# A planner that reckons TensorE's clock from its own order, and passes that shift the priorities of kinds of pieces

## The chip, the cores and the metric

The kernel runs on one core of one Trainium2 chip. The metric is the device time of one execution in microseconds (us), as the median of several. The core has five instruction queues that run side by side, each in the order in which its instructions were written: PE (TensorE, matrix products and transpositions), DVE (VectorE), ACT (ScalarE), POOL (GpSimd) and SP (SyncE, which here issues the transfers). A queue whose next instruction waits for data holds everything behind it.

## The reference

Sliding-window attention with four sink keys, followed by a gated feed-forward block that mixes over the sequence. Four batches, eight heads, 768 positions, 64 per head; d_model 512, d_ff 1024.

```python
scores = scale * np.matmul(q, k.transpose(0, 1, 3, 2))
keep = is_sink | in_window            # 4 sinks, window of 128
a = softmax(where(keep, scores, -1e9))
x = (a @ v), heads side by side       # B, S, 512
h = np.maximum(x @ w_in, 0.0)
u, v = h[..., :512], h[..., 512:]
v_n = (v - mean) / sqrt(var + 1e-6)
v_s = einsum('ts,bsd->btd', w_spatial, v_n) + b_spatial
out = (u * v_s) @ w_out
```

w_in and w_out come as 64-bit floats and are decoded on the chip. Products are made from halves (a high and a low part of 16 bits, or of a reduced 32-bit type), three matmuls for each.

## The kernel before

The sequence is cut in six tiles t of 128 rows and the heads in two halves hf, so that a batch b has twelve "halves" of attention, 48 in all (counted here from 0: half 0 is b 0, t 0, hf 0). For each half PE makes the scores (tile `sc`, L969 for batch 0 and L975 for the others), DVE masks them and takes the row maximum (L980, writes `pexp`, `nm`), ACT makes the exponentials (L985), and the weights are transposed: in batch 0 on PE (`tr`, L1013; a small one for the sinks at L1022) with a copy to `pT` on ACT or DVE (L1017), in the other batches by a DMA (L1047). Then PE multiplies by v (`av`, L1101 and L1093 in batch 0, L1085 to L1087 in the others). DVE divides (L1112, writes `x`), x is split in two halves and transposed by a DMA (L1129, `xT`). The feed-forward block has four kinds of products on PE, all at L686: `ps_v` (x by the second half of w_in; 12 matmuls, 24 pieces), `ps_u` (the first half; 12 matmuls, 48 pieces), `ps_s` (w_spatial by the normalised v; 18 matmuls, 48 pieces) and `ps_o` (w_out; 12 matmuls, 24 pieces).

At the start the weights are read and decoded: `dec` is the raw w_in, `w` and `wtmp` are its parts on ACT (L741, L743), DVE and POOL put them together (L739 to L752), a maximum over all of w_in (`ps_row`, `ps_col` are the two small PE steps of such a maximum) gives the scale, and `win` are the scaled halves (L654 on ACT, L675 on DVE). `junk` are ACT passes that sum absolute values for the scales of v and w_spatial.

None of this order is written by hand. `Plan` collects the pieces (`add`) with a rank, the engines that may do them, a time for each and the keys that they read and write. `prepare` finds the dependences. `forward` lays the pieces out one after the other in a model of the five queues and the buffers: of the pieces that could go on next it takes the one with the smallest start plus a small penalty for its priority. `backward` goes through the same pieces from the end and returns for each the latest start; these are the priorities of the next pass. `order` repeats this 40 times and keeps the pass with the earliest end. In the model PE's pieces took 1.9 times as long up to a fixed moment, 33:

```python
if e == "PE" and b < COLD:
    d *= COLD_TIMES
```

The instructions are then written out in the order of that pass, and on the chip each queue runs its own share in that order.

Of the kernel before, what the change touches and what calls it, by code (L numbers as in the profile page):

```python
# [299 lines left out]
NAMES = ("PE", "d", "a", "p", "SP")  # L300


class Plan:
# [8 lines left out]

    def add(self, rank, engines, time, f, reads=(), writes=(), dma=None, shared=False):
        self.pieces.append((rank, len(self.pieces), engines, time, f, tuple(reads), tuple(writes), dma, shared))

    def prepare(self):
        ps = self.ps = sorted(self.pieces, key=lambda x: x[:2])
        n = len(ps)
        before, seen, users = [set() for _ in ps], {}, {}
        for i, (_, _, _, _, _, reads, writes, _, _) in enumerate(ps):  # L320
# [36 lines left out]

    def forward(self, prio):
        ps, n = self.ps, len(self.ps)
# [5 lines left out]
        free = dict.fromkeys(NAMES, 0.0)  # L365
        port, moved = 0.0, DMA_START
        open_ = [i for i in range(n) if not missing[i]]
# [18 lines left out]
        while open_:  # L386
            least = min(prio[i] for i in open_)
            best = None
            for i in open_:
                t = room(i)  # L390
                if t is None:
                    continue
                t = max(t, ready[i])
                if ps[i][7] and not ps[i][5]:
                    t = max(t, moved - QUEUED)
                c = None
                for e, d, shared in self.choices[i]:
# [6 lines left out]
                key = (c[1] + min(AHEAD_MOST, AHEAD * (prio[i] - least)), prio[i], i)  # L404
                if best is None or key < best[0]:
                    best = (key, c)
            if best is None:
                raise RuntimeError("plan: no piece can go on: " + str([(ps[i][0], ps[i][5], ps[i][6]) for i in open_[:16]])
                                   + str({r: [(b, b and left[b]) for b in h] for r, h in slots.items()}))
            (_, _, i), (_, t, e, d) = best  # L410
            _, _, _, _, f, reads, writes, dma, shared = ps[i]
# [64 lines left out]

    def order(self):
        self.prepare()
        prio, best, self.ends = [p[0] for p in self.ps], None, []
        for _ in range(PASSES):  # L480
            end = self.forward(prio)
            self.ends.append(end)
            if best is None or end < best[0]:
                best = (end, self.last)
            prio = self.backward()
        self.end, (start, length, lag, engine, order, follow) = best
        return [(self.ps[i][4], engine[i]) for i in order]


# [50 lines left out]
def fast_path(tc, st, scalars, qk, v, v0, vs, w_in, w_sp, b_sp, w_out, out):  # L540
# [7 lines left out]
    with (  # L548
# [149 lines left out]
        def all_max(rank, name, cols):  # L698
# [19 lines left out]
            plan.add(rank, "d", 0.15, a, [("mx", name)], [("m", name)])  # L718
            plan.add(rank, "PE", 0.2, b, [("m", name)], [("ps_row", name)])
            plan.add(rank, "d", 0.27, c, [("ps_row", name)], [("1", name)])  # L720
# [226 lines left out]
        def scores(i, b, t, hf, h2, r, n):  # L947
# [35 lines left out]
            def exped(q):  # L983
# [3 lines left out]
            keys = [(f"kslot{kslot(b, x)}", (b, x)) for x in ((t, t - 1) if t else (t,))]  # L987
            plan.add(r, "PE", 0.19 + n / 2 * (0.45 if whole(b) else 0.35), product,
                     ([("qkraw", (b, t)), ("k0room", 0)] if whole(b) else [("qp", (b, t))]) + keys, banks)
            for q in range(n):  # L990
# [10 lines left out]
        def weights_whole(i, b, t, hf, r):  # L1001
# [4 lines left out]
            for k in range(n // 4):  # L1006
# [11 lines left out]
                plan.add(r, "PE", 0.44, turn, [("pexp", i, h) for h in hs], [("tr", (i, k))])  # L1018
                plan.add(r + WHEN["copy0"], ENGINES["pT copy"], {"a": 0.54, "d": 0.63}, copy, [("tr", (i, k))], [("pT", i, k)])
            if t > 1:  # L1020
# [11 lines left out]
                plan.add(r, "p", 0.17, pick_sinks, [("pexp", i)], [("sk", i)])  # L1032
                plan.add(r, "PE", 0.11, turn_sinks, [("sk", i)], [("tr", (i, "s"))])
                plan.add(r + WHEN["copy0"], ENGINES["pT copy"], {"a": 0.23, "d": 0.22}, copy_sinks, [("tr", (i, "s"))],
# [30 lines left out]
        def attend(i, b, t, hf, r):  # L1065
# [48 lines left out]
            if whole_values(b):  # L1114
                plan.add(r, "PE", (0.55 if t > 1 else 0) + 0.225 * n + 0.15, product_whole, [("pT", i)] + [v_key(kt) for kt in tl_]
                         + ([("sinkT", i), ("p16", ("v", hf), 1)] if t > 1 else []), [("av", (b, t), hf)])
            else:
                plan.add(r, "PE", 0.03 * 3 * n + 0.12, product,
                         [("pT", i)] + vkeys + ([(f"vsink{vsk}", b)] if t > 1 else []), [("av", (b, t), hf)])
            if hf == 0:  # L1120
# [13 lines left out]
        def v_half(b, t, r):  # L1134
# [40 lines left out]
            vn = lambda: tl("vn", i)  # L1175
            plan.add(r, "PE", 2.62, product, [("xT", (b, t // 2), t % 2), ("win", 1)], [("ps_v", i)])
            plan.add(r + WHEN["v relu"], ENGINES["v relu"], {"a": 0.59, "d": 0.6}, relu, [("ps_v", i), ("icv", b)], [("vr", i)])
# [7 lines left out]
        def u_half(b, c0, d, r):  # L1185
# [10 lines left out]

            plan.add(r, "PE", 1.33, product, [("xT", (b, c0)), ("win", 0)], [("ps_u", i)])
            plan.add(r + WHEN["u relu"], "a", 0.36, lambda e: nc.scalar.activation(  # L1198
# [4 lines left out]
        def s_piece(b, c0, d, r):  # L1203
# [20 lines left out]
            g2 = lambda: tl("g2", i)  # L1224
            plan.add(r, "PE", 2.0, product, [("vn", (b, s)) for s in range(NT)] + [("wsp", s) for s in range(NT)], [("ps_s", i)])
            plan.add(r + WHEN["gate"], "d", 0.4, gate, [("ps_s", i), ("b_bc", 0)], [("g", i)])
# [4 lines left out]
        def o_piece(b, c0, k, r):  # L1231
# [11 lines left out]
            r0 = TC * c0 + k * P  # L1243
            plan.add(r, "PE", 2.83, product, [("g2", (b, c0, d)) for d in range(KC)] + [("wout", c) for c in range(KC)], [("ps_o", i)])
            plan.add(r + WHEN["o copy"], "a", 0.5, lambda e: nc.scalar.copy(tl("ob", i), tl("ps_o", i)), [("ps_o", i)], [("ob", i)])  # L1245
# [102 lines left out]
```

## Time and profile before

| | |
|---|---|
| time, median of 3 runs | 441.69 us (440.2 to 443.3) |
| profiled execution, its own time | 440.84 us |
| span of that execution | 439.1 us |
| mean granted clock of TensorE in it | 0.974 |
| PE busy | 417.5 us, 95% of the span |
| DVE busy | 324.0 us, 74% |
| ACT busy | 272.3 us, 62% |
| POOL busy | 174.9 us, 40% |
| DMA | 59.98 MB, mean 137 GB/s |

The span is what lies between the first and the last instruction of the execution; the time has 1.8 us more around it. A busy PE is not PE at its peak: its matmuls take twice as long where the granted clock is 0.50 (1.2 GHz) as where it is 1.00 (2.4 GHz). A granted clock of 0.51 or 0.97 is a mean over a stretch that has some of both. In the trace views a row with "xN" stands for N instructions in a row; the bracket behind it says how long the engine had been idle and what ended that. The fp32 matmuls of batch 0 stand as two instructions each.

### The profile page before, as it was taken

What the parts mean: (1) busy time and instruction counts of PE and PEld (TensorE: products, weight loads), DVE (VectorE), ACT (ScalarE), POOL (GpSimd) and SP (SyncE); (2) the same over time, 40 slices, a digit from 0 to 9 for tenths busy, and PEclk for the clock granted to TensorE, in tenths of its full rate; (3) what the DMA queues carried; (4) which work ended last, traced back from release to release, by engine and by line L of the source; (5) the groups of instructions that cost most, each with busy time, mean ns of one, the idle gap of its engine ahead of it and who ended that gap; (6) DMA issues with size and microseconds to landing.
All of it is one profiled execution on the core that took longest, in us unless ns stands there. A gap on an engine that the chain in (4) does not pass through costs nothing.

```text
span 439.1 us, 9829 instructions
## 1 busy us (share of the span) xinstructions
PE 417.5 (95%) x3669; PEld 327.4 (75%) x3669; DVE 324.0 (74%) x925; ACT 272.3 (62%) x583; POOL 174.9 (40%) x227
## 2 busy tenths in 40 slices
PE   2689999999999999999999999999999999999994
PEld 1467787777877878767778877868778778688883
DVE  1998799869899997779897875779996656144430
ACT  2898979978876765488865554778663443232121
POOL 4324346645865652255536713445531213000000
PEclk9957999969999999999999999999999999999999
DMA  7999721355876845279958664366543614500111
GB/s 212 331 353 311 222 68 30 98 120 158 176 176 157 210 116 173 65 165 229 209 111 176 132 144 115 74 166 167 115 79 100 144 58 56 92 1 13 37 49 55
DMA packets 117928, 59.98 MB, mean 137 GB/s; under 512 B 100240, under 2 KB 103920, under 8 KB 117872
## 3 DMA queue, kind: packets, MB, share of 16 engines
q1 hardware_dynamic: 117872, 59.27, 53.7%
q8 instruction: 31, 0.51, 0.5%
q14 instruction: 25, 0.20, 0.2%
HBM read 28.58 MB, written 6.29 MB: 79 GB/s over the span
## 4 chain that ended last, share of the span: by engine, by line
PE 84%; DVE 8%; DMA 4%; ACT 2%; issue 1%; SPq 0%; DVEq 0%; ACTq 0%
PE ps_s L686 18%; PE ps_o L686 15%; PE ps_u L686 15%; PE ps_v L686 12%; PE sc L975 7%; PE av L1101 5%; PE sc L969 2%; PE tr L1013 2%; DVE pexp L980 2%; PE av L1085 2%; DMA dec<-w_in 2%; PE av L1087 2%; PE av L1086 2%; DMA wsp<-qk_t 1%; PE av L1093 1%; DVE vring L675 1%
## 5 line engine op out<-in xcount | busy, mean ns | idle before, releaser
L686 PE MATMUL ps_s<-wsp,vn 128*128 128x256 f16 x864 | 100.8, 273 | 0.0
L686 PEld LDWEIGHTS <-vn 128*128 128x128 f16 x864 | 82.7, 98 | 12.5 <-issue 0.7
L985 ACT ACTIVATE pexp<-pexp,nm 128x260 f32<-128x260 f32 (+1 forms) x192 | 81.9, 484 | 14.9 <-DVE nm L980 14.8
L686 PE MATMUL ps_o<-wout,g 128*128 128x512 f32 x288 | 71.0, 400 | 0.6 <-DVE g L1219 0.3
L686 PE MATMUL ps_u<-xT,win 128*128 128x256 f16 x576 | 68.9, 273 | 0.5 <-ACT vr L1150 0.5
L686 PE MATMUL ps_v<-win,xT 128*128 128x512 f16 x288 | 66.7, 381 | 0.0
L686 PEld LDWEIGHTS ps_o<-wout,g 128*128 128x128 f32 x288 | 52.9, 188 | 13.9 <-DVE g L1219 0.8
L686 PEld LDWEIGHTS <-win 128*128 128x128 f16 x576 | 54.6, 98 | 10.6 <-issue 2.4
L668 DVE TENSOR_TENSOR p<-pexp,p 128x1024 f16<-128x1024 f32 (+2 forms) x57 | 48.8, 876 | 3.6 <-ACT p L652 2.7
L686 PEld LDWEIGHTS <-xT 128*128 128x128 f16 x288 | 27.2, 98 | 30.8 <-issue 1.8
L1219 DVE SCALAR_TENSOR_TENSOR g<-ps_s,isc,b_bc 128x256 f32<-128x256 f32 x48 | 23.1, 481 | 34.8 <-PE ps_s L686 33.6
L668 POOL TENSOR_TENSOR x<-x,x 128x512 f16<-128x512 f32 x24 | 32.8, 1365 | 34.3 <-ACT x L652 33.8
L652 ACT CAST g<-g 128x256 fp32r<-128x256 f32 x35 | 14.0, 403 | 46.1 <-DVE g L1223 44.4
L975 PE MATMUL sc<-kring,qp 64*128 64x260 f32 (+1 forms) x432 | 36.2, 300 | 0.0
L975 PEld LDWEIGHTS sc<-kring,qp 64*128 64x128 f32 x432 | 28.8, 189 | 7.1 <-issue 4.1
L1198 ACT ACTIVATE u<-ps_u,icu 128x256 f32<-128x256 f32 x48 | 22.6, 470 | 18.0 <-PE ps_u L686 18.0
L1245 ACT COPY ob<-ps_o 128x512 f32<-128x512 f32 x24 | 14.0, 585 | 30.2 <-PE ps_o L686 30.2
L1166 POOL TENSOR_TENSOR rs<-rs,mhalf 128x1 f32<-128x1 f32 x24 | 17.7, 738 | 36.6 <-DVE rs L1160 34.6
L652 ACT CAST p<-pexp 128x1024 f16<-128x1024 f32 (+2 forms) x52 | 31.4, 637 | 0.5
L1156 DVE BATCH_NORM_STATS2 st<-vr 128x6 f32<-128x512 f32 x24 | 16.5, 690 | 18.2 <-ACT vr L1150 18.2
L1085 PE MATMUL av<-vring,pT 128*128 128x65 f16 x264 | 27.7, 193 | 0.0
L1086 PE MATMUL av<-vring,pT 128*128 128x65 f16 x264 | 27.6, 193 | 0.0
(151 smaller groups left out, 773.9 us busy)
## 6 DMA issues: line engine op xcount, KB each, us to landing
qkraw<-qk_t SPq DMA_DIRECT2D x18, 512.0 KB, 4.4
out<-ob SPq DMA_DIRECT2D x24, 256.0 KB, 2.2
vraw<-v_s SPq DMA_DIRECT2D x18, 256.0 KB, 4.5
dec<-w_in SPq DMA_DIRECT2D x8, 512.0 KB, 8.4
dec<-w_out SPq DMA_DIRECT2D x4, 512.0 KB, 5.6
wsp<-qk_t SPq DMA_DIRECT2D x6, 256.0 KB, 6.1
qkraw<-qk_t SPq DMA_DIRECT2D x6, 256.0 KB, 4.0
wsp<-w_sp_t SPq DMA_DIRECT2D x3, 384.0 KB, 9.5
```

The lines of the kernel that those rows point to most:

```text
L652: nc.scalar.copy(o, x)
L668: eng[e].tensor_tensor(out=o, in0=x, in1=hi, op=ALU.subtract)
L686: nc.tensor.matmul(o, a, m, start=(i == 0), stop=(i == n - 1))
L975: nc.tensor.matmul(o, qp[rows, qi, hp, :], keys(kring[:, ki], rows), start=(m == 0), stop=(m == 2))
L985: nc.scalar.activation(po, po, AF.Exp, bias=nm()[:, h2 + q:h2 + q + 1], scale=-1.0)
L1085: nc.tensor.matmul(o[:, h], ph, vh, start=(t < 2 and j == 0), stop=False)
L1086: nc.tensor.matmul(o[:, h], ph, vl, start=False, stop=False)
L1101: nc.tensor.matmul(o[:, h], pT[:, q * P:(q + 1) * P], v_whole(kt)[:, g:g + D + 1], start=(t < 2 and j == 0), stop=(j == nb - 1 and (t < 2 ...
L1156: nc.vector.bn_stats(s6, vr())
L1166: nc.gpsimd.tensor_tensor(out=vals["rs", i], in0=vals["rs", i], in1=mhalf, op=ALU.pow)
L1198: plan.add(r + WHEN["u relu"], "a", 0.36, lambda e: nc.scalar.activation(tl("u", (b, c0))[:, d, :], tl("ps_u", i)[:, :TC], AF.Relu, scale= ...
L1219: nc.vector.scalar_tensor_tensor(out=g(), in0=tl("ps_s", i)[:, :TC], scalar=vals["s", "sp"][1], in1=b_bc[:, t0:t0 + TC], op0=ALU.mult, op1 ...
```

## The change

Three things are changed, all in the planner; no operation of the kernel is added or taken away.

- A class `Clock` stands in for the fixed moment. `add` takes the moving columns of each PE piece, `forward` hands each piece that it lays out on PE to the clock, and the clock says for the next whether it runs at full or half speed (factor 2.0).
- `order` no longer repeats 40 like passes and takes the best. It goes through 22 steps. Each step runs some passes, and the first pass of a step adds to every priority a pseudo-random shift, one for each kind of piece and one for each piece, from a seed in the table. The order is that of the last pass. If a pass gets stuck, `settle` repeats it with a stronger pull to the priorities.
- The model times of scores on PE are changed: in batch 0 from 1.09 to 1.10 (0.62 for t 0), in the others from 0.89 to 0.93 (0.79 for t 0).

```diff
-COLD, COLD_TIMES, DMA_START, DMA_LAND = 33.0, 1.9, 0.5, 1.5
+COLD_TIMES, DMA_START, DMA_LAND = 2.0, 0.5, 1.5
+SPELL, ENOUGH = 3.41333, 3030.0
-PASSES = 40
+PASSES = ((3000009, 582, 0, 4), (3000010, 417, 0, 3), (3000020, 470, 158, 4),
...
+class Clock:
+    def __init__(self):
+        self.start, self.sum, self.full = -SPELL, 0.0, False
+    def at(self, t):
+        start, sum_, full = self.start, self.sum, self.full
+        while start + SPELL <= t:
+            start, sum_, full = start + SPELL, 0.0, sum_ >= ENOUGH
+        return start, sum_, full
+    def time(self, t, d):
+        return d if self.at(t)[2] else d * COLD_TIMES
+    def run(self, t, d, columns):
+        self.start, self.sum, self.full = self.at(t)
+        end, p = t + d, t
+        while end > self.start + SPELL:
+            q = self.start + SPELL - p
+            self.full = self.sum + columns * q / d >= ENOUGH
+            p = self.start = self.start + SPELL
+            self.sum = 0.0
+        self.sum += columns * (end - p) / d
+def scatter(seed, i):
+    x = (seed * 2654435761 + i * 40503 + 12345) & 0xFFFFFFFF
...
+    return (x & 0xFFFF) / 65536.0 + (x >> 16) / 65536.0 - 1.0
...
-                    if e == "PE" and b < COLD:
-                        d *= COLD_TIMES
+                    if e == "PE":
+                        d = clock.time(b, d)
...
+            if e == "PE":
+                clock.run(t, d, columns)
...
+        self.end = self.settle([p[0] for p in self.ps])
+        for seed, of_kind, of_piece, passes in PASSES:
+            for k in range(passes):
+                prio = self.backward()
+                if k == 0:
+                    prio = [x + of_kind / 100.0 * scatter(seed, kind[p[1]]) + of_piece / 100.0 * scatter(seed + 7919, 100000 + p[1])
+                            for x, p in zip(prio, self.ps)]
+                self.end = self.settle(prio)
+        start, length, lag, engine, order, follow = self.last
...
+    def settle(self, prio):
+        ahead, most = AHEAD, AHEAD_MOST
+        while True:
+            try:
+                return self.forward(prio, ahead, most)
+            except Stuck:
+                ahead, most = 2 * ahead, 4 * most
...
```

What this does to the program is a new order on every queue, and another engine for some of the pieces that may go to several. Three places follow.

The first is ACT at the start of the program, before the change (w and wtmp are the decode of w_in, pexp the exponentials):

```order
L741 ACTIVATE w_181<-dec 128x512
L743 ACTIVATE wtmp<-dec 128x512
L985 ACTIVATE pexp<-pexp,nm 128x128 x4
L741 ACTIVATE w_207<-dec 128x512
L741 ACTIVATE w_211<-dec 128x512
L743 ACTIVATE wtmp<-dec 128x512
L985 ACTIVATE pexp<-pexp,nm 128x128 x4
```

And with the change:

```order
L1046 ACTIVATE pexp<-pexp,nm 128x128 x4
L802 ACTIVATE w_200<-dec 128x512
L804 ACTIVATE wtmp<-dec 128x512
L1046 ACTIVATE pexp<-pexp,nm 128x128
L802 ACTIVATE w_217<-dec 128x512
L1046 ACTIVATE pexp<-pexp,nm 128x128
L1079 COPY pT<-tr 128x512
```

The exponentials of half 0 moved ahead of the first decode; those of half 1 stay behind it.

The second is SP at the start, before the change (`wsp` holds k of batch 0 at that time, `qkraw` its q):

```order
L924 DMA wsp<-qk_t 128x4x128
L680 DMA qkraw<-qk_t 128x512
L680 DMA dec<-w_in 128x1024 x3
L924 DMA wsp<-qk_t 128x4x128
L680 DMA qkraw<-qk_t 128x512
L680 DMA dec<-w_in 128x1024
L886 DMA vring<-v_ones 128x2x520 x2
```

And with the change:

```order
L985 DMA wsp<-qk_t 128x4x128
L741 DMA qkraw<-qk_t 128x512 x2
L985 DMA wsp<-qk_t 128x4x128
L741 DMA dec<-w_in 128x1024 x3
L947 DMA vring<-v_ones 128x2x520
L741 DMA dec<-w_in 128x1024
L947 DMA vring<-v_ones 128x2x520
```

The q and k of the second tile, 256 KB each, moved ahead of the first three loads of w_in.

The third is PE up to the first `ps_v`. Before the change, from the transpositions of half 2:

```order
L1013 MATMUL tr<-ident,pexp 128x128 x8
L713 MATMUL ps_col<-allmax_352,ones 128x1
L1101 MATMUL av<-vring,pT 128x65 x4
L969 MATMUL sc<-wsp,qkraw 128x260 x4
L1101 MATMUL av<-vring,pT 128x65 x8
L1013 MATMUL tr<-ident,pexp 128x128 x8
L706 MATMUL ps_row<-ident,allmax_m 1x128
L969 MATMUL sc<-wsp,qkraw 128x260 x4
L1101 MATMUL av<-vring,pT 128x65 x8
L1013 MATMUL tr<-ident,pexp 128x128 x8
L1022 MATMUL tr<-ident,sk 16x128
L686 LDWEIGHTS xT
```

And with the change, from the transpositions of half 3:

```order
L1075 MATMUL tr<-ident,pexp 128x128 x8
L1030 MATMUL sc<-wsp,qkraw 128x260 x4
L1163 MATMUL av<-vring,pT 128x65 x8
L1075 MATMUL tr<-ident,pexp 128x128 x8
L767 MATMUL ps_row<-ident,allmax_m 1x128
L1084 MATMUL tr<-ident,sk 16x128
L1163 MATMUL av<-vring,pT 128x65 x8
L1030 MATMUL sc<-wsp,qkraw 128x260 x4
L1075 MATMUL tr<-ident,pexp 128x128 x8
L1084 MATMUL tr<-ident,sk 16x128
L747 LDWEIGHTS xT
```

Before the first `ps_v` now stand the scores of seven halves where six stood, and the transpositions of half 5 as well; the scores of half 5 come ahead of the `av` of half 2, and both `ps_row` that came one by one ahead of half 2's transpositions (not in these rows) now come together.

## Rows read from the trace of the kernel before

**Rows 1.** The page: busy time of the engines with its share of the span and instruction counts, GB/s moved in 40 slices of 11 us, and the shares of the engines in the chain that ended last.

```profile
PE 417.5 (95%) x3669; PEld 327.4 (75%) x3669; DVE 324.0 (74%) x925; ACT 272.3 (62%) x583; POOL 174.9 (40%) x227
GB/s 212 331 353 311 222 68 30 98 120 158 176 176 157 210 116 173 65 165 229 209 111 176 132 144 115 74 166 167 115 79 100 144 58 56 92 1 13 37 49 55
PE 84%; DVE 8%; DMA 4%; ACT 2%; issue 1%; SPq 0%; DVEq 0%; ACTq 0%
```

**Rows 2.** Busy time by stretch, cut where the granted clock changes: the stretch and its length, busy us (and instructions) of PE, of PE's weight loads, of DVE, ACT and POOL, then the granted clock, the DMA share and GB/s.

```profile
17.00:23.90 6.90, 3.59 (x23) 2.43 (x22) 6.73 (x24) 5.86 (x14) 3.95 (x4) 1.00 0.90 270
23.90:37.50 13.60, 13.43 (x58) 11.23 (x60) 13.13 (x43) 12.36 (x24) 2.66 (x3) 0.50 1.10 321
44.00:92.10 48.10, 48.10 (x354) 36.48 (x355) 43.35 (x143) 43.23 (x95) 26.44 (x39) 1.00 0.39 107
92.10:99.00 6.90, 6.90 (x33) 5.30 (x33) 3.68 (x14) 4.54 (x11) 2.80 (x4) 0.51 0.40 102
99.00:121.00 22.00, 22.00 (x244) 17.12 (x243) 20.18 (x55) 19.26 (x43) 15.64 (x15) 1.00 0.69 170
121.00:165.00 44.00, 42.93 (x420) 33.05 (x418) 43.15 (x106) 30.00 (x69) 27.05 (x30) 1.00 0.68 165
165.00:434.00 269.00, 268.37 (x2477) 213.26 (x2475) 181.81 (x502) 142.84 (x303) 86.88 (x98) 1.00 0.48 110
```

**Rows 3.** ACT in order of time, the first 45 us: start, length, line, operation, tiles, and in the bracket the idle time ahead.

```profile
9.39 0.66 ACT L741 ACTIVATE w<-dec 128x512 f32<-128x512 f32 x1 [7.17 <-DMA dec<-w_in]
9.96 0.64 ACT L743 ACTIVATE wtmp<-dec 128x512 int32<-128x512 uint32 x1
10.51 1.27 ACT L985 ACTIVATE pexp<-pexp,nm 128x128 f32<-128x128 f32 x4
11.67 1.22 ACT L741 ACTIVATE w<-dec 128x512 f32<-128x512 f32 x2
...
18.71 1.06 ACT L845 ACTIVATE junk<-vring 128x1024 bf16<-128x1024 f32 x1 [0.15 <-POOL w L752]
...
21.61 0.61 ACT L845 ACTIVATE junk<-p 128x512 bf16<-128x512 f32 x1
...
26.05 0.91 ACT L985 ACTIVATE pexp<-pexp,nm 128x260 f32<-128x260 f32 x2
26.87 1.32 ACT L654 ACTIVATE win<-w,win_scale 128x512 f16<-128x512 f32 x2
...
31.13 1.72 ACT L985 ACTIVATE pexp<-pexp,nm 128x260 f32<-128x260 f32 x4 [0.15 <-DVE nm L980]
...
38.05 1.72 ACT L985 ACTIVATE pexp<-pexp,nm 128x260 f32<-128x260 f32 x4
40.44 1.07 ACT L1017 COPY pT<-tr 128x512 f32<-128x512 f32 x2 [0.67 <-PE tr L1013]
41.39 0.63 ACT L652 CAST x<-x 128x512 f16<-128x512 f32 x1
41.91 0.85 ACT L790 ACTIVATE junk<-wsp 128x768 bf16<-128x768 f32 x1
```

**Rows 4.** PE in order of time, the first 60 us.

```profile
4.83 2.70 PE L969 MATMUL sc<-wsp,qkraw 64*128 64x128 f32 x16 [4.83 <-DMA qkraw<-qk_t]
13.41 1.09 PE L1013 MATMUL tr<-ident,pexp 128*128 128x128 f32 x4 [5.88 <-POOL w L752]
...
24.01 0.37 PE L706 MATMUL ps_row<-ident,allmax_m 128*1 128x128 f32 x1 [2.53 <-DVE allmax_m L703]
...
28.73 2.10 PE L969 MATMUL sc<-wsp,qkraw 64*128 64x260 f32 x8
30.77 3.67 PE L1101 MATMUL av<-vring,pT 128*128 128x65 f32 x16
34.24 1.91 PE L1013 MATMUL tr<-ident,pexp 128*128 128x128 f32 x8
...
40.78 2.75 PE L686 MATMUL ps_v<-win,xT 128*128 128x512 f16 x12
43.90 1.15 PE L969 MATMUL sc<-wsp,qkraw 64*128 64x260 f32 x8 [0.37 <-DMA wsp<-qk_t]
44.98 0.38 PE L713 MATMUL ps_col<-allmax,ones 1*128 1x1 f32 x2
...
50.20 2.76 PE L686 MATMUL ps_v<-win,xT 128*128 128x512 f16 x12
52.80 1.04 PE L1013 MATMUL tr<-ident,pexp 128*128 128x128 f32 x8
...
54.51 2.00 PE L1101 MATMUL av<-vring,pT 128*128 128x65 f32 x16
56.44 1.15 PE L969 MATMUL sc<-wsp,qkraw 64*128 64x260 f32 x8
```

**Rows 5.** PE in order of time, 84 to 100 us.

```profile
88.86 2.00 PE L1101 MATMUL av<-p,pT 128*128 128x65 f32 x16
90.78 0.89 PE L975 MATMUL sc<-kring,qp 64*128 64x128 f32 x12
...
91.84 0.94 PE L1093 MATMUL av<-p 16*128 16x260 f32 x2
92.71 3.67 PE L1101 MATMUL av<-p,pT 128*128 128x65 f32 x16
```

More of the change, by code (lines that the diff above doesn't have):

```diff
@@ L311, in __init__, with add @@
         self.pieces, self.rings, self.ring_of = [], rings, ring_of
-    def add(self, rank, engines, time, f, reads=(), writes=(), dma=None, shared=False):
-        self.pieces.append((rank, len(self.pieces), engines, time, f, tuple(reads), tuple(writes), dma, shared))
+    def add(self, rank, engines, time, f, reads=(), writes=(), dma=None, shared=False, columns=0):
+        self.pieces.append((rank, len(self.pieces), engines, time, f, tuple(reads), tuple(writes), dma, shared, columns))
     def prepare(self):
@@ L319, in prepare @@
         before, seen, users = [set() for _ in ps], {}, {}
[L320 removed]
+        for i, (_, _, _, _, _, reads, writes, _, _, _) in enumerate(ps):
             for key, wr in [(k, False) for k in reads] + [(k, True) for k in writes]:
@@ L356, in prepare, with forward @@
             self.choices.append([(e, p[3][e] if isinstance(p[3], dict) else p[3], e == "p" or (e == "d" and p[8])) for e in es])
-    def forward(self, prio):
+    def forward(self, prio, ahead, most):
         ps, n = self.ps, len(self.ps)
@@ L365, in forward @@
         free = dict.fromkeys(NAMES, 0.0)
-        port, moved = 0.0, DMA_START
+        port, moved, clock = 0.0, DMA_START, Clock()
         open_ = [i for i in range(n) if not missing[i]]
@@ L403, in forward @@
                         c = x
-                key = (c[1] + min(AHEAD_MOST, AHEAD * (prio[i] - least)), prio[i], i)
+                key = (c[1] + min(most, ahead * (prio[i] - least)), prio[i], i)
                 if best is None or key < best[0]:
@@ L407, in forward @@
             if best is None:
-                raise RuntimeError("plan: no piece can go on: " + str([(ps[i][0], ps[i][5], ps[i][6]) for i in open_[:16]])
+                raise Stuck("plan: no piece can go on: " + str([(ps[i][0], ps[i][5], ps[i][6]) for i in open_[:16]])
                                    + str({r: [(b, b and left[b]) for b in h] for r, h in slots.items()}))
             (_, _, i), (_, t, e, d) = best
-            _, _, _, _, f, reads, writes, dma, shared = ps[i]
+            _, _, _, _, f, reads, writes, dma, shared, columns = ps[i]
             if e == "p" or (e == "d" and shared):
@@ L478, in order @@
         self.prepare()
[L479 to L486, printed above, removed]
-        return [(self.ps[i][4], engine[i]) for i in order]
+        kinds, kind = {}, {}
+        for p in self.pieces:
+            name, which = ((p[6] or p[5])[0])[:2]
+            key = name, str(which[0] if isinstance(which, tuple) else which), p[2] if isinstance(p[2], str) else ""
+            kind[p[1]] = kinds.setdefault(key, len(kinds))
+        self.end = self.settle([p[0] for p in self.ps])
[7 more added lines that the diff above has]
+        start, length, lag, engine, order, follow = self.last
+        return [(self.ps[i][4], engine[i]) for i in order]
+    def settle(self, prio):
[5 more added lines that the diff above has]
+                ahead, most = 2 * ahead, 4 * most
+                if most > 1e6:
+                    raise
 class Begin:
@@ L718, in all_max @@
             plan.add(rank, "d", 0.15, a, [("mx", name)], [("m", name)])
-            plan.add(rank, "PE", 0.2, b, [("m", name)], [("ps_row", name)])
+            plan.add(rank, "PE", 0.2, b, [("m", name)], [("ps_row", name)], columns=256)
             plan.add(rank, "d", 0.27, c, [("ps_row", name)], [("1", name)])
@@ L987, in scores @@
             keys = [(f"kslot{kslot(b, x)}", (b, x)) for x in ((t, t - 1) if t else (t,))]
-            plan.add(r, "PE", 0.19 + n / 2 * (0.45 if whole(b) else 0.35), product,
-                     ([("qkraw", (b, t)), ("k0room", 0)] if whole(b) else [("qp", (b, t))]) + keys, banks)
+            plan.add(r, "PE", (0.06 + n / 4 * (1.04 if t else 0.56)) if whole(b) else 0.19 + n / 2 * (0.37 if t else 0.3), product,
+                     ([("qkraw", (b, t)), ("k0room", 0)] if whole(b) else [("qp", (b, t))]) + keys, banks,
+                     columns=n * (260 if t else 128) * (2 if whole(b) else 1.5))
             for q in range(n):
@@ L1017, in copy @@
                     nc.scalar.copy(o, x) if e == "a" else nc.vector.tensor_copy(o, x)
-                plan.add(r, "PE", 0.44, turn, [("pexp", i, h) for h in hs], [("tr", (i, k))])
+                plan.add(r, "PE", 0.44, turn, [("pexp", i, h) for h in hs], [("tr", (i, k))], columns=1024)
                 plan.add(r + WHEN["copy0"], ENGINES["pT copy"], {"a": 0.54, "d": 0.63}, copy, [("tr", (i, k))], [("pT", i, k)])
@@ L1032, in weights_whole @@
                 plan.add(r, "p", 0.17, pick_sinks, [("pexp", i)], [("sk", i)])
-                plan.add(r, "PE", 0.11, turn_sinks, [("sk", i)], [("tr", (i, "s"))])
+                plan.add(r, "PE", 0.11, turn_sinks, [("sk", i)], [("tr", (i, "s"))], columns=256)
                 plan.add(r + WHEN["copy0"], ENGINES["pT copy"], {"a": 0.23, "d": 0.22}, copy_sinks, [("tr", (i, "s"))],
@@ L1175, in v_half @@
             vn = lambda: tl("vn", i)
-            plan.add(r, "PE", 2.62, product, [("xT", (b, t // 2), t % 2), ("win", 1)], [("ps_v", i)])
+            plan.add(r, "PE", 2.62, product, [("xT", (b, t // 2), t % 2), ("win", 1)], [("ps_v", i)], columns=6144)
             plan.add(r + WHEN["v relu"], ENGINES["v relu"], {"a": 0.59, "d": 0.6}, relu, [("ps_v", i), ("icv", b)], [("vr", i)])
@@ L1195, in product @@
                 three(tl("ps_u", i)[:, :TC], pairs)
-            plan.add(r, "PE", 1.33, product, [("xT", (b, c0)), ("win", 0)], [("ps_u", i)])
+            plan.add(r, "PE", 1.33, product, [("xT", (b, c0)), ("win", 0)], [("ps_u", i)], columns=3072)
             plan.add(r + WHEN["u relu"], "a", 0.36, lambda e: nc.scalar.activation(
@@ L1224, in s_piece @@
             g2 = lambda: tl("g2", i)
-            plan.add(r, "PE", 2.0, product, [("vn", (b, s)) for s in range(NT)] + [("wsp", s) for s in range(NT)], [("ps_s", i)])
+            plan.add(r, "PE", 2.0, product, [("vn", (b, s)) for s in range(NT)] + [("wsp", s) for s in range(NT)], [("ps_s", i)], columns=4608)
             plan.add(r + WHEN["gate"], "d", 0.4, gate, [("ps_s", i), ("b_bc", 0)], [("g", i)])
@@ L1243, in o_piece @@
             r0 = TC * c0 + k * P
-            plan.add(r, "PE", 2.83, product, [("g2", (b, c0, d)) for d in range(KC)] + [("wout", c) for c in range(KC)], [("ps_o", i)])
+            plan.add(r, "PE", 2.83, product, [("g2", (b, c0, d)) for d in range(KC)] + [("wout", c) for c in range(KC)], [("ps_o", i)], columns=6144)
             plan.add(r + WHEN["o copy"], "a", 0.5, lambda e: nc.scalar.copy(tl("ob", i), tl("ps_o", i)), [("ps_o", i)], [("ob", i)])
```

14 lines of the change are left out of this document (12 added, 2 removed).

## The prediction

> **What bounds the kernel now.** I read the page first, then the stages, then the queues of the first 45 us. The page shows PE busy for 95% of the span and on 84% of the chain that ended last; no other engine has more than 8% of that chain [rows 1]. So time is won only where PE idles, runs at half its clock, or is held by another engine. The stages say where that is [rows 2]. From 44 us on PE is busy for all but 1.7 us: it idles 1.07 us between 121 and 165 us (42.93 of 44.00), where DVE is busy for 43.15 us, and 0.63 us after that. Once the granted clock falls to its lower level (1.2 GHz), 92.1 to 99.0 us: PE is busy all through at a mean of 0.51, so half of the 6.9 us, 3.4 us, is lost. The rest of the loss lies before 44 us. In 17.0 to 23.9 us PE does 3.59 us of work in 6.90; from 23.9 to 37.5 us it is busy for 13.43 of 13.60 us, but at 0.50.
>
> Why the start is slow stands in the queues. ACT waits 7.17 us for the first piece of w_in, and the exponentials of half 0, which need nothing of it, stand behind that decode and begin at 10.51 [rows 3]. PE ends its first scores at 7.53 and then idles 5.88 us [rows 4]. Later a `ps_row` waits 2.53 us at the head of PE's queue for a maximum on DVE, and the clock falls right at the end of that wait, at 23.9 [rows 2, 4]. From then on ACT (12.36 of 13.60) and DVE (13.13) are as full as PE [rows 2].
>
> **The change part by part.** Nothing is computed more or less, so each term is a wait that goes, stays or comes.
>
> *Loads and ACT at the start.* The q and k of tile 1 (512 KB) now go ahead of w_in. At 212 to 331 GB/s, the first two slices [rows 1], that is 1.5 to 2.4 us; I take 2.0, so the first decode begins at 9.39 + 2.0 = 11.4. The exponentials of half 0 fill the wait. I then count ACT's queue as it now stands, from that decode to the exponentials of half 5, with steps from the starts of neighbouring rows [rows 3]: 8 `w` at 0.57 (4.6), 5 `wtmp` at 0.55 (2.8), 4 small exponentials at 0.29 (1.2), 16 large ones at 0.41 (6.6), 2 + 2 sums for v at 1.06 and 0.61 (3.3), 6 `pT` copies at 0.48 (2.9), one x at 0.52, 2 sums for w_spatial at 0.85 (1.7), 4 `win` at 0.66 (2.6). That is 26.1 us, so they end at 37.5. Before, the same exponentials ended at 38.05 + 1.72 = 39.8. That is a lead of 2.3 us although the loads are later, because work of less use (the rest of w_in, its scale) went behind.
>
> *PE up to the first `ps_v`.* With the clock at its upper level PE follows these exponentials: 0.2 to be told, 1.0 for the transpositions of half 5 (the row at 52.80), 2.6 for `ps_v` (50.20 to 52.80): 41.3 [rows 4]. Before, PE is through the first `ps_v` and the scores of half 6 at 44.98 [rows 4]; the new order has done both by 41.3, and the transpositions of half 5 (1.0) as well. The lead is 44.98 - 41.3 + 1.0 = 4.7 us. PE is busy from there on as before, so the lead goes straight to the end.
>
> With the clock at its lower level up to 37.5, as before, PE is the last instead. The exponentials of half 3 end at 26.2 by the same count (14.8 us of ACT after 11.4). Then follow, at the lengths of the lower level [rows 4], transpositions (1.7), scores (2.04), `av` (3.47), transpositions (1.9): 35.5. The next `av` gets 2.0 us at half and 0.8 at full clock: 38.3; scores 1.08, transpositions 1.0 and `ps_v` 2.6 end at 43.0. The lead is 3.0 us. I take the middle of 4.7 and 3.0, **3.8 us**: the wait of 2.53 us after which the clock fell is no longer at the head of PE's queue by itself, but PE still has gaps that ACT sets. The bound below: ACT idled 1.24 us of 13.60 [rows 2], 9%, which the count leaves out; on 26.1 us that is 2.4 us more, and 0.6 us of lead is left with the low clock. DVE, as full as ACT, could be the last in its place; the same bound stands for that.
>
> *The fall at 92 us.* Ahead of it PE ran `av`, scores of a first tile, and the next sinks and `av` in a row, all with few columns [rows 5]. The new order has the same run of pieces: `av`, the scores of batch 1's second half, `av`, then `ps_v`. I put it at nothing, with a gain of 3.4 us (no fall) at one end and nothing at the other.
>
> The plan's clock counts from the plan's own zero, so it knows on which pieces a fall will land only if the chip counts likewise. The Trainium skill (TensorE: Matmul & The Clock Gate, "What's actually happening") says that the chip's monitor runs freely and does not start afresh with a kernel. By that rule the order can make a fall less likely but not place it, and this term would be 0 or -3.4 by chance, execution by execution; the trace of one execution cannot show which, and the sum above takes 0 without it.
>
> *121 to 165 us.* DVE is full there. The choice between engines moves little: over the whole program DVE has 913 instructions in place of 920, ACT 568 for 558, POOL 229 for 232 (counted in the orders). So the stretch is as long as before for DVE, and PE comes to it 3.8 us sooner. DVE idled 4.75 us in 44.0 to 92.1 and 1.82 in 99 to 121 [rows 2], which is room for that. I put it at nothing; at one end the 1.07 us of PE's idle goes, at the other DVE has no use for the earlier start and the whole 3.8 is lost here.
>
> *The end.* Both orders finish with products of w_out behind the last `ps_s`, and the last copy and store are the same: nothing, within 1 us.
>
> **Sum.** The profiled execution took 440.84 us for its span of 439.1. 440.84 - 3.8 = **437.0 us**. The three runs have a median of 441.69 (440.2 to 443.3), so the profiled execution is 0.2% below it and I leave the sum as it is. About 1%, 4.4 us, is what a measurement of this kernel can tell from no change; 437.3 is where "faster" begins. The forecast lies just beyond it.
>
> **Rivals.**
> - *The start gives little.* ACT or DVE, not the order, sets the pace, and the low clock stays: a lead of 0.6 to 2.5 us, 438.3 to 440.2. For it: both are over 90% busy in 23.9 to 37.5 [rows 2], and later loads of w_in hold all that stands behind the decode. Against it: 7.17 us of ACT's wait is filled. Chance 0.30.
> - *The clock does not fall at 92 us.* Then 3.4 us go on top of the 3.8: 433.6. For it: it hangs on a run of pieces only 7.5 us long (88.86 to 96.3) [rows 5], so a little less idling may do. Against: the run is the same. Chance 0.14.
> - *Slower: attention comes late in the middle.* Counted along PE's order with the lengths of the rows, the new order puts some scores of batches 1 and 2 by 13 and 23 us of PE work later, and for one half leaves only 10 us of it between scores and `av`, where masks, exponentials, splits and a transfer must run. In 121 to 165 us DVE has 0.85 us to spare [rows 2]. If PE must wait for it by a fifth of those 44 us, 8.8 us, the time is 437.0 + 8.8 = 445.8; from a twelfth on (3.8 us) the whole gain is gone. For it: that stretch already stops PE. Against: DVE's work is the same, and PE's stops are 2% now. Chance 0.12.
> - *The forecast*, 435.5 to 438.3: chance 0.44.
>
> **How the numbers follow.** Faster by over 1% (below 437.3): the third without a fall, 0.14, and three quarters of the forecast's case, 0.33: 0.47. Slower by over 1% (above 446.1): nearly half of the slower rival and a margin for the single mechanism I may have missed: 0.10. Within 1%: 0.43. The range: the low end holds the case without a fall (433.6) with the full lead of 4.7 (432.7); the high end takes in the start that gives little and the spread of the runs above it (1.6 us above the median), 442.0. Left out are most of the slower rival and a tenth of the others.
>
> **What the profile after would show.** Right: ACT's first exponentials begin near 6 us, and the first decode near 11.4; the exponentials of half 5 end near 37.5; the first `ps_v` ends near 41 to 43, with the scores of half 6 and the transpositions of half 5 already done; the low clock is left before 37.5 us; from 45 us on PE is busy in every stretch but 121 to 165. Wrong: the first decode later than 14 us; PE idle for more than 3 us in all after 45 us; a second fall of the clock; or PE waiting for `av` behind transfers of `pT`, which is the slower rival.

## The result, and the profile after

The changed kernel takes 446.02 us (median of 4 runs, 444.96 to 446.88) where the kernel before takes 441.09 (4 runs, 440.2 to 443.3): a ratio of 1.0103, 95% interval 1.0057 to 1.0149. It is slower by 1%, where 437.0 us and a range up to 442.0 had been forecast. Its profiled execution took 444.96 us for a span of 443.2. Here and below the ratios, unlike medians and ranges, leave out runs that took over 1.5% more than the fastest of their kernel.

The page of the changed kernel, busy time of the engines, to set beside [rows 1]:

```profile
PE 422.0 (95%) x3669; PEld 329.0 (74%) x3669; DVE 312.6 (71%) x918; ACT 281.1 (63%) x593; POOL 167.5 (38%) x224
```

PE issues the same 3669 matmul instructions and is busy 4.5 us longer, so some of them ran slower. Where, the stretches tell (columns as in [rows 2]):

```profile
26.50:37.50 11.00, 10.46 (x82) 8.63 (x81) 9.84 (x43) 10.88 (x23) 2.94 (x6) 1.00 0.66 214
37.50:47.00 9.50, 5.55 (x33) 3.15 (x31) 7.92 (x23) 9.50 (x27) 4.20 (x5) 1.00 0.85 272
47.00:60.70 13.70, 13.70 (x57) 10.94 (x57) 5.72 (x25) 5.43 (x13) 2.75 (x6) 0.50 0.36 98
60.70:88.00 27.30, 27.30 (x210) 21.34 (x209) 22.40 (x74) 25.60 (x53) 13.77 (x21) 1.00 0.31 97
88.00:102.00 14.00, 14.00 (x76) 9.10 (x75) 11.87 (x33) 11.46 (x25) 7.63 (x10) 0.76 0.33 68
121.00:165.00 44.00, 44.00 (x469) 35.23 (x467) 40.52 (x112) 33.44 (x73) 28.89 (x32) 1.00 0.65 149
165.00:438.00 273.00, 272.67 (x2524) 215.59 (x2522) 184.85 (x518) 150.32 (x315) 85.04 (x100) 1.00 0.51 114
```

From 37.5 to 47.0 PE does 5.55 us of work in 9.50. From 47.0 to 60.7 it is busy all the time, but at the lower level of its clock (0.50): 13.70 us in which 6.8 us of work at full clock get done. The middle, 121 to 165 us, is better than before: busy 44.00 of 44.00. What stands at the entrance of the bad stretch shows in PE's order of time (the first two rows, from the start, are read further below):

```profile
21.35 2.10 PE L1030 MATMUL sc<-wsp,qkraw 64*128 64x260 f32 x8 [3.55 <-DMA wsp<-qk_t]
...
26.87 1.15 PE L1030 MATMUL sc<-wsp,qkraw 64*128 64x260 f32 x8
...
36.42 1.15 PE L1030 MATMUL sc<-wsp,qkraw 64*128 64x260 f32 x8
38.56 1.09 PE L1075 MATMUL tr<-ident,pexp 128*128 128x128 f32 x8 [0.99 <-DVE nm L1041]
39.49 0.27 PE L1084 MATMUL tr<-ident,sk 128*16 128x128 f32 x1
39.60 2.75 PE L747 MATMUL ps_v<-win,xT 128*128 128x512 f16 x12
45.31 1.15 PE L1030 MATMUL sc<-wsp,qkraw 64*128 64x260 f32 x8 [2.95 <-DMA wsp<-qk_t]
46.39 0.73 PE L1155 MATMUL av<-p 16*128 16x260 f32 x2
47.05 3.68 PE L1163 MATMUL av<-vring,pT 128*128 128x65 f32 x16
...
58.26 2.10 PE L1030 MATMUL sc<-wsp,qkraw 64*128 64x260 f32 x8
60.30 2.89 PE L747 MATMUL ps_v<-win,xT 128*128 128x512 f16 x12
```

The first `ps_v` is over at 42.3, as forecast. The scores of half 7 (tile 3) stand next and wait 2.95 us for a load of keys. Behind them 16 instructions of `av` take 3.68 us; in [rows 4] 16 like them take 2.00 (at 54.51). The load stands in SP's queue:

```profile
37.11 1.03 SPq L741 DMA_DIRECT2D dec<-w_out  x2
38.23 0.55 SPq L985 DMA_DIRECT2D wsp<-qk_t  x1
```

The one issued at 38.23 brings the keys of tile 5, which the scores of half 7 do not read. They read tiles 2 and 3. In `k_whole` tile t of batch 0 lies in slot 2(t % 2) + (t // 2) % 2: tile 2 in slot 1, tile 3 in slot 3, tile 5 in slot 2. The scores take both slots in one strided slice, `ring[rows, pair[0]:pair[1] + 1:step, hp, :]`, that is slots 1 and 3 in steps of 2, and slot 2 lies inside its span. The plan's pieces name only the two tiles, so the plan could put the load ahead of the scores without seeing a wait.

**Theory A**: the wait comes from this span alone; it costs its 2.95 us and, through the clock that falls behind it, 13.65 / 2 = 6.8 us more. **Theory B**: the attention products bring the clock down anyway, and only the wait can be had back. **Theory C**: ACT or VectorE holds PE there in any case.

### The profile page after: what moved, and what is told of

Read it like the earlier page. It is cut to its first block, busy times and chain, and to the rows that moved or that the text cites. A ratio compares the mean times of both kernels' runs of the same rounds, so it can differ in the third digit from the quotient of the medians.

```text
span 443.2 us, 9852 instructions
## 1 busy us (share of the span) xinstructions
PE 422.0 (95%) x3669; PEld 329.0 (74%) x3669; DVE 312.6 (71%) x918; ACT 281.1 (63%) x593; POOL 167.5 (38%) x224
## 4 chain that ended last, share of the span: by engine, by line
PE 90%; DMA 5%; DVE 2%; SPq 1%; ACT 0%; issue 0%; ACTq 0%
PE ps_s L747 22%; PE ps_o L747 15%; PE ps_u L747 15%; PE ps_v L747 14%; PE sc L1036 7%; PE av L1163 5%; DMA wsp<-qk_t 3%; PE sc L1030 2%; PE tr L1075 2%; PE av L1147 2%; PE av L1148 2%; PE av L1149 2%; DMA dec<-w_in 2%; PE av L1155 1%; SPq L741 1%; PE av L1141 1%
## 5 line engine op out<-in xcount | busy, mean ns | idle before, releaser
L747 PE MATMUL ps_s<-wsp,vn 128*128 128x256 f16 x864 | 99.5, 273 | 0.0
L747 PE MATMUL ps_o<-wout,g 128*128 128x512 f32 x288 | 72.2, 402 | 0.0
L747 PE MATMUL ps_v<-win,xT 128*128 128x512 f16 x288 | 68.7, 390 | 0.0
L729 DVE TENSOR_TENSOR p<-pexp,p 128x1024 f16<-128x1024 f32 (+2 forms) x57 | 44.8, 795 | 8.7 <-ACT p L713 8.5
L729 POOL TENSOR_TENSOR x<-x,x 128x512 f16<-128x512 f32 x24 | 29.3, 1222 | 32.8 <-ACT x L713 31.9
L1283 DVE SCALAR_TENSOR_TENSOR g<-ps_s,isc,b_bc 128x256 f32<-128x256 f32 x48 | 23.1, 482 | 23.9 <-PE ps_s L747 22.4
L713 ACT CAST g<-g 128x256 fp32r<-128x256 f32 x32 | 12.9, 404 | 41.1 <-DVE g L1287 36.5
L713 ACT CAST p<-pexp 128x1024 f16<-128x1024 f32 (+2 forms) x56 | 34.9, 651 | 1.1 <-DMA pT<-p 0.4
L1030 PE MATMUL sc<-wsp,qkraw 64*128 64x260 f32 (+1 forms) x96 | 18.7, 484 | 11.5 <-DMA wsp<-qk_t 6.5
L1214 ACT ACTIVATE vr<-ps_v,icv 128x512 f32<-128x512 f32 x24 | 16.4, 685 | 19.3 <-PE ps_v L747 17.5
L722 POOL TENSOR_SCALAR g<-g 128x256 fp32r<-128x256 f32 x16 | 8.4, 524 | 52.5 <-PE ps_o L747 22.3
```

The costliest lines, as they stand in the source:

```text
L729: eng[e].tensor_tensor(out=o, in0=x, in1=hi, op=ALU.subtract)
L747: nc.tensor.matmul(o, a, m, start=(i == 0), stop=(i == n - 1))
L1030: nc.tensor.matmul(o, tl("qkraw", (b, t))[rows, 0, hp, :], keys(k_whole, rows), start=True, stop=True)
L1214: nc.scalar.activation(vr(), tl("ps_v", i), AF.Relu, scale=ic)
L1283: nc.vector.scalar_tensor_tensor(out=g(), in0=tl("ps_s", i)[:, :TC], scalar=vals["s", "sp"][1], in1=b_bc[:, t0:t0 + TC], op0=ALU.mult, op1 ...
```

## The experiments

Where a piece is moved, it is moved in the list that the plan has ordered, just before the list is issued: `behind` and `ahead_of` take out SP's entry for a load and put it back behind or ahead of another piece, `forward_to` does so with an entry of PE. The helper functions shift the line numbers (the scores are L1044 with the loads moved, L1051 with a `ps_v` moved too, L969 in the kernel before and L983 there with a load moved).

**The load of tile 5 moved** behind the scores of half 7 (e1_k5_behind):

```diff
         order = plan.order()
+        behind(order, ("kslot2", (0, 5), 0), ("dec", ("out", 0, 2)))
```

> The changed kernel with one SP entry moved: the load of the keys of tile 5 (batch 0) goes from ahead of the scores of half 7 to behind them and behind the third load of w_out. Theory A (the scores of half 7 read the slots of tiles 2 and 3, but their strided slice spans the slot into which tile 5 is loaded, so they wait 2.95 us for a transfer that they don't read, and the idle lets the clock fall for the 13.65 us that follow): the scores of half 7 start near 42.4 instead of 45.31 with no wait for the keys, the 13.65 us of low clock behind them are gone, about 2.95 + 6.8 = 9.7 us come back in that place, less what later stages take again: 436 to 439 us. Theory B (the clock falls there anyway, since the attention products behind the scores are small): the wait goes, the low stretch stays, 442 to 444 us. Theory C (another engine holds TensorE there, the keys only came last): the scores stand until near 45 with another releaser, 445 to 447 us.

Measured: 435.85 us (434.11 to 439.99, 12 runs), ratio to the kernel before 0.9900 [0.9868, 0.9931]. PE in order of time, then two stretches:

```profile
38.52 2.75 PE L761 MATMUL ps_v<-win,xT 128*128 128x512 f16 x12
41.20 1.15 PE L1044 MATMUL sc<-wsp,qkraw 64*128 64x260 f32 x8
42.28 0.70 PE L1169 MATMUL av<-p 16*128 16x260 f32 x2
42.91 2.00 PE L1177 MATMUL av<-vring,pT 128*128 128x65 f32 x16
```

```profile
38.00:62.00 24.00, 23.94 (x164) 16.91 (x162) 22.63 (x73) 23.63 (x58) 9.69 (x12) 1.00 0.62 179
80.00:104.00 24.00, 24.00 (x171) 16.59 (x170) 18.13 (x51) 19.54 (x43) 14.95 (x17) 0.86 0.53 127
```

No bracket stands at the scores, and from 38 to 62 us PE does 164 matmul instructions at full clock (the changed kernel 93, at a mean of 0.72). One moved load is worth 446.02 - 435.85 = 10.2 us in time and, since the two medians come from different sets of runs, 2.0% or about 9 us by the two ratios; A said 9.7. Theories B and C fall.

**The idle filled, the wait left** (e4_v_twice):

```diff
-                three(tl("ps_v", i), pairs)
+                for _ in range(2 if i == (0, 0) else 1):
+                    three(tl("ps_v", i), pairs)
```

> The changed kernel, waits as they are, but the first ps_v (tile 0 of batch 0) is computed twice into the same bank: 2.6 us of work of TensorE in the 2.95 us in which it stood still ahead of the scores of half 7. Theory A (the idle is what brings the clock down): the scores of half 7 still start near 45.3, but the clock does not fall at 47; 6.8 us come back, 438 to 441 us. Theory B (the attention products bring it down): the clock falls at 47 as before, 445 to 447 us.

Measured: 438.64 us (436.13 to 441.77, 10 runs), ratio 0.9943 [0.9907, 0.9980].

```profile
40.25 5.34 PE L747 MATMUL ps_v<-win,xT 128*128 128x512 f16 x24
45.84 1.15 PE L1030 MATMUL sc<-wsp,qkraw 64*128 64x260 f32 x8 [0.25 <-DVE allmax L771]
46.92 0.70 PE L1155 MATMUL av<-p 16*128 16x260 f32 x2
47.55 2.00 PE L1163 MATMUL av<-vring,pT 128*128 128x65 f32 x16
```

The scores begin no earlier than in the changed kernel, and 2.6 us of useless work went in, yet 7.4 us come back: the products behind run at full clock. So the two parts of the loss are told apart, about 3 us for the wait and about 7 for the clock, and in the changed kernel it is the idle time that brings the clock down there.

**The load left, the slice split** (e5_split_read): the products of half 7 are split in two, one slot each (its four products stand as eight instructions and become sixteen; the expectation counts instructions).

```diff
+                            if i == 7:
+                                for j, sl in enumerate(pair):
+                                    nc.tensor.matmul(o[:, j], tl("qkraw", (b, t))[rows, 0, hp, :],
+                                                     k_whole[rows, sl, hp, :], start=True, stop=True)
+                                continue
```

> The changed kernel with every load where the change put it; only the scores of half 7 are written otherwise: each of their 8 products over a strided slice of two key slots (260 columns) becomes two products over one slot each (130 columns), so that no slice spans the slot into which the keys of tile 5 are loaded. Theory A (the wait comes from the span of the slice alone): the scores of half 7 start near 42.4 without a wait for the keys, no low stretch at 47; up to 0.6 us more work than in e1_k5_behind: 435 to 438 us. Rival (the wait comes from the transfer's place in the queue, or from another reader of it): the scores still wait until about 45, 445 to 447 us.

Measured: 437.72 us (434.13 to 439.44, 4 runs), ratio 0.9889 [0.9826, 0.9952].

```profile
40.17 2.75 PE L747 MATMUL ps_v<-win,xT 128*128 128x512 f16 x12
42.85 1.27 PE L1032 MATMUL sc<-wsp,qkraw 64*128 64x130 f32 x16
```

With every load where the change put it, the wait is gone: it came from the span of the slice. The sixteen `av` instructions behind the scores take 2.00 us, at full clock. Split, the scores cost 1.27 us for 1.15.

**The same loss made in the kernel before** (e6_before_k5_late): there the scores of half 6 (tile 3 too) wait 0.37 us for the same load [rows 4].

```diff
         order = plan.order()
+        behind(order, ("kslot2", (0, 5), 0), ("wraw", 3))
```

> The kernel before with one SP entry moved: the load of the keys of tile 5, for which the scores of half 6 wait 0.37 us there, goes behind the load of w_sp that is issued at 42.1, so that it is issued near 42.5 instead of 38.48 and lands near 47. Theory A: the scores of half 6 wait 3 to 4 us behind the first ps_v, the clock falls behind them and stays low for 10 us or more while the attention products and transpositions run, and the kernel before loses what the changed one lost: 3.5 + 5 to 7 us, 447 to 452 us. Theory B (idle time of TensorE costs only itself): 443 to 445 us, no low stretch between 40 and 60.

Measured: 447.05 us (445.37 to 452.59, 4 runs), ratio 1.0105 [1.0049, 1.0161].

```profile
40.47 2.75 PE L700 MATMUL ps_v<-win,xT 128*128 128x512 f16 x12
48.18 2.10 PE L983 MATMUL sc<-wsp,qkraw 64*128 64x260 f32 x8 [4.95 <-DMA wsp<-qk_t]
...
51.80 3.67 PE L1115 MATMUL av<-vring,pT 128*128 128x65 f32 x16
```

The profiled run, the longest of the four, repeats the picture: a wait of 4.95 us, and half clock from 46.4 to 60.8 (the rows at 48.18 and 51.80; in [rows 4] such rows take 1.15 us at 43.90 and 2.00 at 54.51). The other three, 445.37 to 448.19, lie 3.7 to 6.5 us above the kernel before's 441.68 of that chip; their median of 445.9 falls between the two theories' ranges, and the longer wait alone (4.95 for 0.37 us) would give 4.6. Whether the clock fell behind it in them too, no trace shows, and their mean granted clock (0.982 to 0.986, against 0.972 in the profiled one) can't tell, since it says neither where the clock was low nor anything of the time ahead of a trace's first fall (last section). So it is shown that the late load costs the kernel before 1%, as much as the whole change; that the clock falls with the wait there is seen in one execution, the slowest. In the order of the changed kernel the fall seems to come each time: its four runs have a mean clock of 0.969 to 0.977, the twelve of e1_k5_behind 0.988 to 0.996. What makes it surer there stays open.

**The load of tile 2** (e2_k2_ahead), for which the scores of half 3 wait 3.55 us at 21.35 in the changed kernel, and both moves together (e3_both):

```diff
+        ahead_of(order, ("kslot1", (0, 2), 0), ("dec", ("in", 0, 1)))
```

> The changed kernel with one SP entry moved: the load of the keys of tile 2 goes ahead of the load of w_in that holds SP from 8.1 to 13.7 us, so that it lands before the scores of half 3 that wait 3.55 us for it at 21.35 without reading it. The wait in the middle of the run (k of tile 5) stays. Theory A (only idle time behind the start costs; here the decoding on ACT and VectorE holds the start): the scores of half 3 start near 18, the first ps_v still ends between 41 and 43, the low stretch at 47 stays, 444 to 447 us. Rival (TensorE's idle time at the start is on the path): up to 3.5 us come back, 442 to 444 us.

> The moves of e1_k5_behind and e2_k2_ahead together. Theory A: as e1_k5_behind within 1 us, 435 to 439 us. If both waits are on the path the gains add: 1 to 3.5 us less than e1_k5_behind. Theory C: 444 to 447 us.

Measured: 445.95 us (10 runs, ratio 1.0105 [1.0073, 1.0137]) alone, 434.28 (6 runs, 0.9873 [0.9820, 0.9926]) together. Alone it brings nothing in the median: the scores of half 3 begin 1.5 us sooner, at 19.85, released by VectorE now and no longer by the load, and the low stretch behind the first `ps_v` is still there. But its ten runs stand in two groups, 443.3 to 444.8 and 447.1 to 448.3 us, and the trace is one of the second: eight scores still take 2.10 us in it at 30.58, at half clock, where those of the changed kernel take 1.15 at 26.87. A clock that rises later can hide an earlier start, so whether that idle time at the start is on the path stays open. Between these two kernels, on one chip, only the load of tile 5 differs: 445.95 - 434.28 = 11.7 us, near the 10.2 above.

**`ps_v` between the attention products** (e8_v_between): e3_both, and the `ps_v` of tile 3 goes ahead of the scores of half 13, between the `av` of halves 10 and 11.

```diff
+        forward_to(order, ("ps_v", (0, 3)), ("sc", (13, 0)))
```

> e3_both with one TensorE piece moved: the ps_v of tile 3 (batch 0) goes from behind the attention products of half 11 to ahead of the scores of half 12, so that the two groups of attention products at 82 and 85 us no longer follow each other. Theory A: the clock fell at 86 because of what ran from 80 to 87.6 (transpositions, attention products, scores, all busy, no idle); with the ps_v between them it does not fall, 1.7 us (3.4 us at half speed) come back: 431.5 to 434 us. Rival (the fall does not hang on the order of these pieces, or the attention products moved back by 2.6 us hold VectorE's division and a later ps_v): same as e3_both or slower, 434 to 437 us.

(It calls the scores of half 13 those of half 12.) Measured: 434.78 us (431.38 to 437.01, 6 runs), ratio 0.9844 [0.9797, 0.9891]. The stretch around the fall, of e3_both and then of this kernel:

```profile
80.00:104.00 24.00, 24.00 (x178) 16.51 (x177) 19.52 (x52) 21.21 (x45) 15.58 (x17) 0.93 0.58 134
```

```profile
80.00:104.00 24.00, 23.46 (x195) 16.53 (x194) 20.83 (x52) 21.40 (x47) 15.03 (x17) 1.00 0.68 143
```

The fall is gone (0.93 x 24 us leaves 1.7 us lost, 1.00 none), but six runs of each could not show the gain; the median lies in the rival's range. So both, and e1_k5_behind, ran again side by side:

> e8_v_between again, beside e3_both on one chip, since six runs of each did not tell them apart. If the fall of the clock near 86 us costs its 1.7 us, this is 1 to 3 us faster than e3_both; if something else stands behind that fall, they are the same within 1 us.

> e3_both again, beside e8_v_between: 433 to 436 us; the fall of the clock near 86 us is in the profiled run again.

> e1_k5_behind again on the same chip: if the load of the keys of tile 2 counts (the idle time at the start is on the path), e3_both is 1 to 3 us faster than this; if not, they are the same within 1 us: 434 to 437 us.

Measured: 432.95 us (0.9839 [0.9798, 0.9879]), 435.86 (0.9881 [0.9836, 0.9926]; 435.02 without one run of 441.83) and 436.19 (0.9904 [0.9869, 0.9939]). The traces repeat the picture: from 80 to 104 us the clock is 1.00 in e9_v_between_again and 0.93 in e10_both_again. Over both sets the medians are 434.0 us (12 runs), 435.0 (12) and 435.9 (19): the steps lie in the expected order, and their intervals overlap, so neither the second fall nor the load of tile 2 has a proven price. All three beat both kernels; the best is 1.6% below the kernel before.

**The rule alone** (e7_rule_alone): the clock rule, the columns and the new score times with 40 plain passes, the best kept.

```diff
-PASSES = ((3000009, 582, 0, 4), ...
+PASSES = ((0, 0, 0, 39),)
...
+        best = self.end, self.last
...
+                best = min(best, (self.end, self.last), key=lambda x: x[0])
...
```

> The clock rule and the new score times without the shifts: 40 plain passes of which the best is kept, as in the kernel before. If the gain at the start comes from the shifted passes, the first ps_v ends near 43.5 as in the kernel before and the time is 439 to 443 us; if the rule alone brings it, the first ps_v ends near 42 and, without the wait for the keys of tile 5 (its scores of half 7 stand 45 pieces behind that load), 434 to 439 us.

Measured: 440.97 us (10 runs), ratio 0.9968 [0.9936, 0.9999]: neither case, with the time of the first and a `ps_v` earlier than in the second.

```profile
39.60 0.59 PE L749 MATMUL ps_v<-win,xT 128*128 128x512 f16 x2 [0.88 <-DVE win L738]
...
42.84 0.70 PE L1157 MATMUL av<-p 16*128 16x260 f32 x2 [1.25 <-DVE x L1176]
...
48.32 1.23 PE L1032 MATMUL sc<-wsp,qkraw 64*128 64x260 f32 x2 [1.26 <-ACT pT L1081]
...
51.45 3.68 PE L1165 MATMUL av<-vring,pT 128*128 128x65 f32 x16
```

The first `ps_v` is over at 40.2, as early as in any trace here, so an early start comes without the shifted passes, in this execution at least. But PE then runs ahead of VectorE and ACT, waits three times, and the clock falls here too. e1_k5_behind, which has the shifted passes, neither these waits nor that fall, stands at 0.9900; where in the run its 0.7% more come from was not taken apart further.

## Why the prediction was wrong

*Loads and ACT at the start: right in the end, by two misses that offset each other.* The first exponentials start at 5.96 us (forecast near 6). The first decode starts at 8.13, not 11.4: the two loads ahead of w_in cost it nothing, where the prediction had put 2.0 us. From there to the end of the exponentials of half 5, at 38.4 (forecast 37.5, before 39.8), ACT takes 30.3 us where 26.1 were counted. It is busy for 26.7 of them, so the count of work was good; the 3.5 us in which ACT waits were left out of it and stood only in the lower bound (2.4 us).

```profile
5.96 1.29 ACT L1046 ACTIVATE pexp<-pexp,nm 128x128 f32<-128x128 f32 x4 [3.74 <-DVE nm L1041]
8.13 0.67 ACT L802 ACTIVATE w<-dec 128x512 f32<-128x512 f32 x1 [0.88 <-DMA dec<-w_in]
...
37.11 1.30 ACT L1046 ACTIVATE pexp<-pexp,nm 128x260 f32<-128x260 f32 x3
```

*PE up to the first `ps_v`: right in size, and partly by luck.* It ends at 42.3 with the scores of half 6 and the transpositions of half 5 done: by the prediction's own formula 44.98 - 42.3 + 1.0 = 3.7 us of lead, 3.8 forecast. The 3.8 was the middle between a high and a low clock, but in this execution eight scores take 1.15 us from 26.87 on: it is the case of the high clock, 4.7 us, less the 0.9 us by which ACT came later. With the clock low up to about 38 us, as in e9_v_between_again (last section), the first `ps_v` ends at 45.7, where the prediction's case of the low clock has 43.0, and the same formula leaves 0.3 us of lead.

*The step that failed* is the sentence behind it: "PE is busy from there on as before, so the lead goes straight to the end." No wait was counted between the first `ps_v` and the middle. There the lead met the transfer of tile 5's keys, 2.95 us, and then 6.8 us of half clock, 9.8 in all against 3.7 won. The sign was in [rows 4]: the scores of half 6 at 43.90 waited 0.37 us "<-DMA wsp<-qk_t", for a tile that they do not read. The prediction says nothing of it; it is a dependency that the plan does not know and that a shifted order can make longer. The new places of the loads were weighed for ACT's decodes, not for PE's scores.

*The fall at 92 us: right in size.* There are two falls instead of one; the row of 88 to 102 us at 0.76 gives 14.0 x 0.24 = 3.4 us, as before.

*121 to 165 us: the good end.* PE's idle time of 1.07 us is gone; it was put at nothing.

*The sum.* 440.84 - 3.7 + 2.95 + 6.8 - 1.07 = 445.8 us, against 444.96 in the profiled execution and 446.02 in the median. Without the wait and its clock it would be 436.1; e1_k5_behind has 435.85.

*The rivals.* The one that ended slower had named 445.8 us too, but for another reason, PE waiting for `av` in 121 to 165 us, and that stretch became better. That the start gives little did not happen. Among the kept traces, 80 to 112 us passed without a fall only with a `ps_v` put between the attention products, and in e7_rule_alone, which has another order. Of the signs named as "wrong" only a second fall of the clock is there. The long wait of PE ends at 45.31, so it lies just ahead of 45 us; behind that PE idles for 0.6 us in all up to 438, and the sign "from 45 us on PE is busy" is met by a kernel that is slower: a PE at half clock is busy too.

## What to carry to other kernels

A wait in the trace for a tile that the instruction does not read is a dependency that an order written by a plan does not know: find the slice that spans it, however short the wait, before moving loads. Give the plan the span as it is tracked, move the load behind the reader, or read the slots one by one. Idle time of TensorE in mid-run can cost more than itself through the clock behind it: here 2.95 us cost some 10. It need not: in e5_split_read the second `ps_v` waits 1.52 us, and eight transpositions behind it take 1.04 us, at full clock.

## What the runs showed of the hardware

The clock stayed at its lower level for 13.6 us although PE was busy 13.70 of 13.70 us, with scores, transpositions and attention products; it came back near 60.6, as the next `ps_v` had begun (60.30). The Trainium skill (TensorE: Matmul & The Clock Gate, "HAM oscillation — how this bites in real kernels") tells of stretches that start at half clock because the engine had waited for a transfer. This trace agrees in kind, with 2.95 us of waiting ahead of it, just under the waits of about 3 to 5 us in the skill's example; but the scores right behind the wait still ran at full clock (1.15 us at 45.31), and the fall came at 47.0. Waiting is not needed for a fall: ahead of the one at 92.1 us in the kernel before PE was busy 48.10 of 48.10 us [rows 2].

The clock column reads 1.00 up to the first fall that a trace shows, whatever the clock is. In the changed kernel too it reads 1.00 at 21.35, where eight scores take 2.10 us, and at 26.87, where they take 1.15: the clock rose in between. Two executions of one program show it best, e8_v_between and e9_v_between_again, both "1.00" from 20 to 38 us:

```profile
20.00:38.00 18.00, 16.63 (x116) 13.31 (x116) 16.39 (x68) 18.00 (x40) 4.61 (x9) 1.00 0.92 321
```

```profile
20.00:38.00 18.00, 17.70 (x78) 14.18 (x77) 13.04 (x54) 12.98 (x27) 4.98 (x7) 1.00 0.79 271
```

```profile
25.67 2.11 PE L1051 MATMUL sc<-wsp,qkraw 64*128 64x260 f32 x8
...
36.05 1.91 PE L1096 MATMUL tr<-ident,pexp 128*128 128x128 f32 x8
...
43.02 2.75 PE L768 MATMUL ps_v<-win,xT 128*128 128x512 f16 x12
```

The second, of which the last rows are, does 78 instructions in 17.70 us where the first does 116 in 16.63; eight scores take 2.11 us, against 1.15 at full clock. Its first `ps_v` ends 5.5 us later (45.7 for 40.2), and its span is 436.2 us for 429.5. So how early the clock rises differs from execution to execution of the same order, and between these two that makes up most of the 6.7 us. That it also stands behind the spread of the other runs, 5 to 7 us in most of these kernels, is likely, but they have no traces. And two mean granted clocks can't be compared where one trace shows a fall at the start and the other none: the kernel before has 0.50 from 23.9 to 37.5 us [rows 2], e6_before_k5_late, the same program up to there, reads 1.00 from 20 to 40, though sixteen `av` instructions take 3.65 us in it at 30.83.
